# State products as 64 by 64 tiles with crossed heads, gates fetched first, single stores, weight sums on VectorE, and a new order

## The chip, the cores and the metric

One Trainium2 chip, one of its cores. The metric is the device time of one execution in microseconds (us). The matrix engine (TensorE) is called PE here, its weight loads PEld; VectorE is DVE, ScalarE is ACT, GpSimdE is POOL, and SP is the engine whose queue issues nearly all DMAs.

## What is computed

A gated linear recurrence with a complex gate (four sequences of 768 tokens, eight heads of 48), and behind it a feed-forward layer with a squared ReLU:

```python
mag = np.sqrt(a_re * a_re + a_im * a_im)
scale = np.minimum(mag, 0.999) / (mag + 1e-06)
a_re_n, a_im_n = (a_re * scale, a_im * scale)
for t in range(S):
    new_re = ar * S_re - ai * S_im
    new_im = ar * S_im + ai * S_re
    kv = np.einsum('bhd,bhe->bhde', k[:, :, t], v[:, :, t])
    S_re, S_im = (new_re + kv, new_im)
    y[:, :, t] = np.einsum('bhd,bhde->bhe', q[:, :, t], S_re)
x = y.transpose(0, 2, 1, 3).reshape(B * S, H * D)     # 3072 x 384
h = np.maximum(x @ w_in, 0.0)                          # w_in 384 x 2048
return (h * h @ w_out).astype(np.float32)              # w_out 2048 x 384
```

The weights arrive in 64-bit floating point, everything else in 32-bit.

## The kernel before

**Tiles and stages.** The tokens are cut into 24 chunks of 128. Two chunks of two sequences form a group; there are 12 groups (`NGR`), and groups 0 and 6 hold first chunks of their sequences, 5 and 11 last ones. Eight heads stand as four pairs (`NP`), the two heads of a pair on partitions 0 to 47 and 64 to 111; the fourth pair lies in the gap rows of the other three and is moved out by small DMAs.

**What a group needs.** `load_parts` (token `l`) fetches gates, queries and keys into the one buffer `raw` by 16 DMAs, `load_values` (`v`) the values. `make_operands` (`o0` to `o21`) turns gates into running quotients: ACT and DVE by turns, ending in `products` (four multiplications that write `qk`) and `last_heads` (six DMAs). `chunk` (`a` and `b`, one for each chunk of the group) makes the attention: `scores` (products of the queries with the state, L810, then the scores of keys and queries, L817, then six transposes of the keys, L824), `turned_keys` (ACT copies them), `masked` (DVE), `sums_of_values` (L845), `tokens` (ACT copies the result to `x`), `added` (L860), `new_state` (DVE) and `state_operand` (ACT spreads the new state over `state_mm`, which has zeros beside each head so that one 128-wide product does both heads of a pair). `fill_gaps` (`g`) moves the fourth pair's part of `x` into the gap rows by two DMAs, and then the feed-forward begins: eight `first_product` (`F`, L902), each followed by `squared_relu` on ACT (`H`).

**The second product.** For group 0 it is the plain one (`S`, then `E`, L918). For groups 1 to 11 it is done with seven half products in place of eight (`Z`, L975), for which DVE forms sums of the hidden values (`X`, `Y`, `Q`) and puts the results together (`R`, which also issues the stores of the output on SP in its steps 5 and 6). The sums of the weights that this needs are made once by `sum_weights` (`t`) on POOL.

**The weights.** They come as 16 blocks: `fetch` (`f`) loads one into one of three buffers, `weights` (`D`) turns it into 32-bit floats by five DVE instructions, `watch` (`W`) has ACT look at its size. The string `order` says that blocks of the first and the second matrix alternate. A feed-forward block `F` of any group needs one block of the first matrix.

**What sets the order.** The string `FRONT` is the whole order, written out token by token. The instructions of PE, DVE, ACT and SP stand on their queues exactly in that order, and each engine does its own in order; POOL is left to the scheduler. PSUM has eight banks: two each for `a_ps`, `m` (transposes and `add`) and `h`, one each for `y` and `o_ps`. A path for unusual inputs follows; it is not run here.

## Time and profile before

| | us |
|---|---|
| median of 3 runs | 794.98 (793.86 to 795.91) |
| the profiled execution, its own time | 796.23 |
| its span | 794.5 |
| PE busy | 648.3 (82%) |
| DVE busy | 544.5 (69%) |
| ACT busy | 380.9 (48%) |
| POOL busy | 25.1 (3%) |

The span is what the profiler covers from the first to the last instruction; the execution's own time is 1.7 us longer. A 32-bit matmul appears as two records, so 48 first products of a group are 96 records. A record's duration is a latency, and records overlap: what one costs in a row of many is read from the chain of waits, where a line gives the time that a run of them held the chain. The granted clock of PE is given as a share of full speed, 1.00 for 2.4 GHz and 0.50 for 1.2 GHz.

### The profile page before, as it was taken

The numbers are of one execution on the slowest core, as the hardware profiler recorded it, in microseconds if no ns is written. First come the engines' busy times: TensorE is split into PE (matmuls) and PEld (weight loads), VectorE is DVE, ScalarE is ACT, GpSimd is POOL, SyncE is SP. The second block draws the span as 40 slices with busy tenths as digits, with TensorE's granted clock in tenths as the row PEclk, the third lists the DMA queues.
The fourth block names the chain that finished last, engine by engine and source line by source line (L and its number), as shares of the span: only waits on it lengthen the run. The fifth ranks groups of instructions, "written<-read, shape, count | busy, mean of one in ns | idle before, by whom it ended". The sixth has DMA issues, their size and how long they took to land.

```text
span 794.5 us, 12035 instructions
## 1 busy us (share of the span) xinstructions
PE 648.3 (82%) x4683; PEld 585.8 (74%) x4683; DVE 544.5 (69%) x1060; ACT 380.9 (48%) x654; POOL 25.1 (3%) x38
## 2 busy tenths in 40 slices
PE   0005396887974999999996999999869979999995
PEld 0004385656974998998995999989859968989995
DVE  2899999999654697777862977868826847833120
ACT  2638547446622934828343646366337266132130
POOL 3000001050000000000000000000000000000000
PEclk9999687998996999999997999999969999999999
DMA  7567694033014143062331061430620510020001
GB/s 166 131 104 155 120 183 99 2 73 64 9 26 79 41 70 60 18 95 70 50 46 31 6 100 41 68 78 2 97 68 2 80 36 11 6 52 16 13 7 26
DMA packets 46019, 47.72 MB, mean 60 GB/s; under 512 B 5888, under 2 KB 40832, under 8 KB 45952
## 3 DMA queue, kind: packets, MB, share of 16 engines
q1 hardware_dynamic: 45440, 46.46, 31.0%
q8 instruction: 39, 0.64, 0.4%
q10 hardware_dynamic: 512, 0.39, 0.2%
q14 instruction: 28, 0.23, 0.1%
HBM read 36.18 MB, written 4.72 MB: 51 GB/s over the span
## 4 chain that ended last, share of the span: by engine, by line
PE 64%; DVE 15%; DMA 10%; ACT 4%; SPq 4%; issue 2%; ACTq 0%; DVEq 0%
PE h_ps L902 29%; PE o_ps L975 21%; DMA raw<-in_feat_dram 5%; PE a_ps L817 4%; PE y L810 4%; PE y L845 3%; DMA x<-x 2%; DVE ab L461 2%; DVE pr L461 2%; PE add L860 2%; PE tp L824 2%; DVE decoded L558 1%; DVE decoded L553 1%; DMA words<-in_moe_w_in_dram 1%; DVE w L461 1%
## 5 line engine op out<-in xcount | busy, mean ns | idle before, releaser
L902 PE MATMUL h_ps<-x,w 128*128 128x256 f32 x1152 | 270.4, 394 | 52.0 <-DMA x<-x 42.4
L902 PEld LDWEIGHTS h_ps<-x,w 128*128 128x128 f32 x1152 | 225.5, 198 | 86.9 <-issue 27.6
L975 PE MATMUL o_ps<-w,h 128*128 128x192 f32 x704 | 120.6, 328 | 0.2 <-DVE h L461 0.2
L975 PEld LDWEIGHTS o_ps<-w,h 128*128 128x128 f32 x704 | 114.6, 190 | 1.5 <-issue 0.7
L907 ACT ACTIVATE h<-h_ps 128x512 f32<-128x512 f32 x96 | 57.2, 596 | 109.4 <-PE h_ps L902 109.3
L817 PE MATMUL a_ps<-qk 48*128 48x128 f32 x576 | 42.2, 297 | 59.3 <-ACT sq L661 59.3
L817 PEld LDWEIGHTS a_ps<-qk 48*128 48x128 f32 x576 | 37.5, 204 | 62.8 <-ACT sq L661 59.6
L461 DVE TENSOR_TENSOR a<-a_ps,mask 128x512 f32<-128x512 f32 x48 | 30.8, 684 | 46.7 <-PE a_ps L817 46.7
L908 ACT ACTIVATE h<-h 128x512 f32<-128x512 f32 x96 | 60.6, 631 | 3.1
L975 PE MATMUL o_ps<-w_sum,mix 128*128 128x192 f32 x352 | 60.4, 327 | 0.0
L975 PEld LDWEIGHTS o_ps<-w_sum,mix 128*128 128x128 f32 x352 | 57.4, 190 | 0.7 <-issue 0.3
L461 DVE TENSOR_TENSOR pr<-ab 128x384 f32<-128x384 f32 x84 | 53.0, 631 | 3.4 <-ACT ab L721 0.9
L641 ACT ACTIVATE qk<-raw 128x768 f32<-128x768 f32 x24 | 36.3, 1529 | 31.4 <-DMA raw<-in_feat_dram 13.6
L461 DVE TENSOR_TENSOR mix<-h 128x256 f32<-128x256 f32 x44 | 18.5, 421 | 47.5 <-ACT h L908 47.5
L461 DVE TENSOR_TENSOR qk<-ab,qk 128x768 f32<-128x768 f32 x48 | 44.9, 956 | 0.8
L461 DVE TENSOR_TENSOR o<-o_ps,o 128x192 f32<-128x192 f32 x33 | 11.5, 354 | 44.3 <-issue 22.3
L829 ACT COPY kt<-tp 128x384 f32<-128x384 f32 x40 | 19.6, 491 | 35.2 <-PE tp L824 35.2
L641 ACT ACTIVATE both<-z 128x768 f32<-128x768 f32 x24 | 35.4, 1566 | 1.8 <-DVE z L692 1.8
L641 ACT ACTIVATE ab<-raw 128x768 f32<-128x768 f32 x24 | 35.8, 1559 | 0.0
L461 DVE TENSOR_TENSOR ab<-pr 128x192 f32<-128x192 f32 x84 | 33.2, 395 | 2.9
L845 PE MATMUL y<-a,vt 128*64 128x128 f32 x384 | 29.0, 291 | 7.5 <-DMA vt<-in_vtok_dram 4.1
L661 ACT ACTIVATE sq<-raw 128x1536 f32<-128x1536 f32 x12 | 17.7, 1478 | 35.0 <-DVE ab L461 18.6
(300 smaller groups left out, 870.0 us busy)
## 6 DMA issues: line engine op xcount, KB each, us to landing
raw<-in_feat_dram SPq DMA_DIRECT2D x44, 288.0 KB
words<-in_moe_w_out_dram SPq DMA_DIRECT2D x8, 768.0 KB
last<-qk SPq DMA_DIRECT2D x72, 64.5 KB
words<-in_moe_w_in_dram SPq DMA_DIRECT2D x16, 288.0 KB
vt<-in_vtok_dram SPq DMA_DIRECT2D x24, 192.0 KB
out_dram<-o SPq DMA_DIRECT2D x24, 192.0 KB
raw<-in_feat_dram SPq DMA_DIRECT2D x132, 32.0 KB
words<-in_moe_w_in_dram SPq DMA_DIRECT2D x16, 96.0 KB
```

The costliest lines, as they stand in the source:

```text
L461: nc.vector.tensor_tensor(out=out, in0=in0, in1=in1, op=op)
L641: nc.scalar.activation(out=out.rearrange("p c j n -> p c n j"), func=AF.Copy, in_=in_.rearrange("p c (n j) -> p c n j", j=L), **kwargs)
L661: nc.scalar.activation(out=tiles["sq"], in_=r[:, A_RE:A_IM + 1], func=AF.Square)
L810: nc.tensor.matmul(y[:, p_], rhs=operand(c, p_, slice(0, P)), lhsT=state_mm[b][:, c, p_].rearrange("p hh e -> p (hh e)"), start=(p_ == 0 a ...
L817: nc.tensor.matmul(ps[hh][:, p_], lhsT=operand(2 + c, p_, rows(hh)), rhs=operand(c, p_, rows(hh)), start=(c == RE), stop=(c == IM))
L824: nc.tensor.transpose(tp[:, g], qk[:, 2 + c, b, g, 0:C], ident)
L829: nc.scalar.copy(out=kt[c][:, 0:NG], in_=tp)
L845: nc.tensor.matmul(y[hh * ROWS:(hh + 1) * ROWS, p_], lhsT=v[:, at:at + ROWS], rhs=tiles["am"][hh][:, p_], start=(first and p_ == 0), stop= ...
L902: nc.tensor.matmul(ps[:, j], lhsT=w1[:, g, (2 * f + j) * P:(2 * f + j + 1) * P], rhs=x_of[i][:, g], start=(g == 0), stop=(g == NG - 1))
L907: nc.scalar.activation(out=h, in_=h_ps[i, f], func=AF.Relu)
L908: nc.scalar.activation(out=h, in_=h, func=AF.Square)
L975: nc.tensor.matmul(to, lhsT=x(k)[:, j], rhs=factors[z][:, 2 * k + j], start=(z in (0, 1, 3) and k == j == 0), stop=(k == KH // 2 - 1 and j ...
```

## The change

- **State products.** The product of queries with the state is no longer one 128-wide instruction for a pair of heads but one of 64 rows by 64 columns for each head. For odd pairs the two heads' outputs are crossed, so that four consecutive instructions use the four quarters of the array; even and odd pairs write two different PSUM tiles `ys`, and `py` has two banks, `pm` one. The state is kept in the layout in which PE reads it, so `state_operand` goes, and `tokens` copies two halves. The rows of the first weight matrix are crossed in the same way when they are fetched, which takes six DMAs instead of four.
- **Transposes.** They leave `scores` and become separate steps (`keys_turned`, `keys_copied`, for the real part and then the imaginary one), which share the one bank of `pm` with `add`.
- **Front.** Gates, values, queries and keys of group 0 are fetched first, the first weight block behind them. All eight blocks of the first matrix come before the eight of the second. Group 1 too gets the plain second product, block by block (`T`).
- **Weight sums.** The four subtractions go from POOL to DVE, as separate steps.
- **Stores.** They leave `R` and `E` and become steps `s`.
- **Order.** `FRONT` is new throughout.

```diff
-    py = ctx.enter_context(tc.tile_pool(name="py", bufs=1, space=PSUM))
-    pm = ctx.enter_context(tc.tile_pool(name="pm", bufs=2, space=PSUM))
+    py = ctx.enter_context(tc.tile_pool(name="py", bufs=2, space=PSUM))
+    pm = ctx.enter_context(tc.tile_pool(name="pm", bufs=1, space=PSUM))
...
+    def crossed(hh, p_):
+        at = (hh ^ p_ % 2) * ROWS
+        return slice(at, at + ROWS)
...
-    order = "1212121212121212"
+    order = "1111111122222222"
...
-            nc.gpsimd.tensor_tensor(out=out_, in0=x, in1=y, op=ALU.subtract)
...
+        tt(w2_sums[i], x, y, ALU.subtract)
...
             if not first:
-                for p_ in range(NP):
+                for two in range(0, NP, 2):
                     for c in (RE, IM):
-                        nc.tensor.matmul(
-                            y[:, p_], rhs=operand(c, p_, slice(0, P)),
-                            lhsT=state_mm[b][:, c, p_].rearrange("p hh e -> p (hh e)"),
-                            start=(p_ == 0 and c == RE), stop=False, skip_group_check=True)
+                        for hh in range(HH):
+                            for p_ in (two, two + 1):
+                                nc.tensor.matmul(
+                                    ys[p_ % 2][crossed(hh, p_), p_ // 2],
+                                    lhsT=states[b][1 - c_seq % 2][rows(hh), c, p_],
+                                    rhs=operand(c, p_, rows(hh)),
+                                    start=(p_ < 2 and c == RE), stop=False, skip_group_check=True)
...
-            nc.scalar.copy(out=x_of[gi][:, :, b * C:(b + 1) * C], in_=tiles["y"])
+            for odd in range(2):
+                nc.scalar.copy(out=x_of[gi][:, odd::2, b * C:(b + 1) * C],
+                               in_=tiles["y"][odd][:, 0:NP // 2])
...
-        def state_operand():
-            for hh in range(HH):
-                nc.scalar.copy(out=state_mm[b][rows(hh), :, :, hh, 0:D], in_=state[n][rows(hh)])
...
+    def store(i, b):
+        nc.sync.dma_start(out=in_turn(out, groups[i][b]), in_=out_of[i, b])
...
-        "M0 f0 D0 W0 l0.0 o0.0 o0.1 o0.3 o0.4 o0.5 o0.2 o0.7 o0.8 o0.10 o0.9 f1 W1 f2 W2 D1 "
+        "M0 l0.0 v0 v1 l0.1 o0.0 o0.3 o0.1 o0.4 o0.5 o0.7 o0.2 f0 o0.8 o0.10 o0.9 o0.11 o0.6 W0 "
```

How the order moves is shown at three places, as the instructions stand on an engine's queue.

**DVE at the last weight block.** First before, then now. `decoded` and `w_59` are a block of the second weight matrix being turned into floats; `a` is masked scores of group 1, `both`, `ab`, `sq` and `raw` gates of group 2 before, and of group 3 now.

```order
L551 TENSOR_SCALAR decoded<-words 128x768
L553 SCALAR_TENSOR_TENSOR decoded<-words,decoded 128x768
L555 TENSOR_SCALAR decoded<-decoded 128x768
L558 SCALAR_TENSOR_TENSOR decoded<-words,decoded 128x768
L461 TENSOR_TENSOR w_59<-decoded 128x768
L461 TENSOR_TENSOR a<-a_ps,mask 128x512 x2
L713 SCALAR_TENSOR_TENSOR both<-both 128x768
L461 TENSOR_TENSOR ab<-ab,both 128x1536
L717 SCALAR_TENSOR_TENSOR sq<-z,sq 128x768
L727 SCALAR_TENSOR_TENSOR sq<-sq 128x128 x6
```

```order
L478 TENSOR_TENSOR sq<-sq 128x768
L714 SCALAR_TENSOR_TENSOR z<-sq,z 128x768
L569 TENSOR_SCALAR decoded<-words 128x768
L571 SCALAR_TENSOR_TENSOR decoded<-words,decoded 128x768
L573 TENSOR_SCALAR decoded<-decoded 128x768
L576 SCALAR_TENSOR_TENSOR decoded<-words,decoded 128x768
L478 TENSOR_TENSOR w_59<-decoded 128x768
L478 TENSOR_TENSOR w_sum<-w_59 128x1536
L735 SCALAR_TENSOR_TENSOR both<-both 128x768
L478 TENSOR_TENSOR ab<-ab,both 128x1536
```

The last block stood before the rest of group 2's operands and the second chunk of group 1; now it stands behind them and behind the first steps of group 3, and the first sum of weights follows it on DVE.

**PE at the second of group 2's chunks, up to that group's first products.** First before, then now, from the last of the new state products on. `y<-qk` and `y<-last` are state products, `a_ps` scores, `tp` transposes, `y<-a` sums of values, `add` what the chunk adds to the state, `o_ps` the second product of group 1, `h_ps` the first product of group 2.

```order
L810 MATMUL y<-qk_125,state_mm_134 128x128 x6
L810 MATMUL y<-last_127,state_mm_134 128x128 x2
L817 MATMUL a_ps<-qk_125 128x128 x12
L817 MATMUL a_ps<-last_127 128x128 x4
L824 MATMUL tp<-ident,qk_125 128x128 x6
L975 MATMUL o_ps<-w_59,h 128x192 x8
L845 MATMUL y<-a,vt_104 64x128 x8
L860 MATMUL add<-vt_104,kt_141 64x48 x8
L860 MATMUL add<-vt_104,kt_142 64x48 x8
L975 MATMUL o_ps<-w_sum,h 128x192 x8
L902 MATMUL h_ps<-x,w_58 128x256 x48
```

```order
L833 MATMUL y<-qk_125,state_134 64x128
L833 MATMUL y<-last_127,state_134 64x128
L841 MATMUL a_ps<-qk_125 128x128 x12
L841 MATMUL a_ps<-last_127 128x128 x4
L848 MATMUL tp<-ident,qk_125 128x128 x6
L867 MATMUL y<-a,vt_103 64x128 x8
L885 MATMUL add<-vt_104,kt_145 64x48 x8
L885 MATMUL add<-vt_104,kt_146 64x48 x8
L923 MATMUL h_ps<-x,w_58 128x256 x36
```

The blocks of group 1's second product that stood between scores and sums of values are gone from here; all of that product now stands ahead of both chunks. Eight 128-wide state products of a chunk have become 16 of 64 columns.

**SP at the gap rows of group 8.** First before, then now. `raw` and `vt` are loads for a later group, `out_dram` stores of the output, `x<-x` the two DMAs that fill the gap rows, `last` the six DMAs of the fourth pair.

```order
L476 DMA raw<-in_feat_dram 48x4x384
L481 DMA raw<-in_feat_dram 16x4x128 x3
L491 DMA vt_103<-in_vtok_dram 128x1x384
L491 DMA vt_104<-in_vtok_dram 128x1x384
L934 DMA out_dram<-o 8x16x384 x2
L896 DMA x<-x 16x3x256 x2
L778 DMA last_128<-qk_126 16x8x129 x6
L491 DMA vt_105<-in_vtok_dram 128x1x384
```

```order
L493 DMA raw<-in_feat_dram 48x4x384
L498 DMA raw<-in_feat_dram 16x4x128 x3
L508 DMA vt_103<-in_vtok_dram 128x1x384
L508 DMA vt_104<-in_vtok_dram 128x1x384
L917 DMA x<-x 16x3x256 x2
L962 DMA out_dram<-o 8x16x384 x2
L800 DMA last_128<-qk_126 16x8x129 x6
```

The fill of the gap rows stood behind two stores of the group before; now it stands ahead of the two stores, still behind the 16 loads of `raw` and the two of `vt`. On PE three half products of the group before (24 of the 128x192 instructions) stand between the fill and the first product that needs it.

## Rows read from the trace of the kernel before

**Rows 1.** Busy time by stage: stretch, then us of each engine, granted clock, DMA.

```profile
0.00:182.00 182.00, 85.40 (x529) 67.78 (x529) 157.81 (x252) 95.16 (x160) 22.58 (x28) 0.91 0.58 116
182.00:248.80 66.80, 50.84 (x420) 46.60 (x421) 40.52 (x84) 30.23 (x52) 0.28 (x1) 0.88 0.24 45
248.80:302.00 53.20, 51.43 (x397) 47.27 (x397) 41.62 (x87) 28.97 (x54) 0.28 (x1) 0.97 0.28 48
302.00:786.20 484.20, 460.60 (x3338) 424.12 (x3338) 304.38 (x638) 226.25 (x390) 1.96 (x8) 0.97 0.23 43
786.20:794.50 8.30, 0.03 (x2) 0.00 (x0) 0.15 (x1) 0.26 (x1) 0.00 (x0) 0.79 0.23 59
```

**Rows 2.** PE's waits from 248 us on: us in total, times, longest.

```profile
PE h_ps L902 <- DMA x<-x: 32.4, 5, 14.8
PE a_ps L817 <- DMA last<-qk: 7.8, 2, 6.8
```

**Rows 3.** Timeline at group 8's gap rows: start, us, instruction, idle before and releaser.

```profile
574.83 1.52 ACT L641 ACTIVATE qk<-raw 128x768 f32<-128x768 f32 x1 [7.92 <-DMA raw<-in_feat_dram]
...
578.91 1.42 SPq L934 DMA_DIRECT2D out_dram<-o  x2
580.38 1.34 SPq L896 DMA_DIRECT2D x<-x  x2
...
583.91 8.45 PE L902 MATMUL h_ps<-x,w 128*128 128x256 f32 x25 [10.07 <-DMA x<-x]
```

**Rows 4.** Busy time by stage, the first 20 us.

```profile
0.00:20.00 20.00, 0.48 (x1) 0.18 (x1) 4.37 (x11) 5.25 (x9) 6.02 (x22) 1.00 0.79 166
```

**Rows 5.** Chain of waits up to 200 us: start, us, what.

```profile
136.93 4.20 DVE sq L674
...
153.57 0.96 DVE w L461
...
166.15 3.70 DVE pr L461
```

**Rows 6.** DVE groups of the operands: busy us, mean ns, idle before.

```profile
L461 DVE TENSOR_TENSOR pr<-ab 128x384 f32<-128x384 f32 x84 | 53.0, 631 | 3.4 <-ACT ab L721 0.9
L461 DVE TENSOR_TENSOR qk<-ab,qk 128x768 f32<-128x768 f32 x48 | 44.9, 956 | 0.8
L461 DVE TENSOR_TENSOR ab<-pr 128x192 f32<-128x192 f32 x84 | 33.2, 395 | 2.9
L727 DVE TENSOR_TENSOR_SCAN sq<-sq 128x128 f32<-128x128 f32 x72 | 24.0, 403 | 0.2
```

**Rows 7.** Chain of waits at group 2's first products.

```profile
248.81 22.38 PE h_ps L902 x96
```

**Rows 8.** Chain of waits later: start, us, PE's runs of records.

```profile
271.19 1.78 PE y L810 x16
272.98 1.99 PE a_ps L817 x32
...
278.37 1.02 PE y L845 x16
...
329.47 2.79 PE h_ps L902 x12
...
353.65 1.07 PE add L860 x32
...
404.22 2.59 PE h_ps L902 x12
406.81 2.60 PE o_ps L975 x16
...
583.91 16.00 PE h_ps L902 x60
```

**Rows 9.** ACT groups of the chunks: busy us, mean ns, idle before.

```profile
L882 ACT COPY state_mm<-state 48x384 f32<-48x384 f32 x40 | 20.3, 507 | 14.0 <-DVE state L461 13.7
L829 ACT COPY kt<-tp 128x384 f32<-128x384 f32 x40 | 19.6, 491 | 35.2 <-PE tp L824 35.2
```

More of the change, by code (lines that the diff above doesn't have):

```diff
@@ L54, in w1_views @@
     rest = w[cut:].rearrange("(hh r g) f -> hh r g f", hh=HH, g=groups)
-    return [(head_rows(hh, d), main[hh]) for hh in range(HH)] + [
-        (gap_rows(hh, d), rest[hh]) for hh in range(HH)]
+    if not crossed:
+        return [(head_rows(hh, d), slice(0, groups), main[hh]) for hh in range(HH)] + [
+            (gap_rows(hh, d), slice(0, groups), rest[hh]) for hh in range(HH)]
+    assert groups % 2
+    return [(head_rows(hh, d), slice(odd, groups, 2), main[hh ^ odd][:, odd::2])
+            for hh in range(HH) for odd in range(2)] + [
+        (gap_rows(hh, d), slice(0, groups), rest[hh ^ groups % 2]) for hh in range(HH)]
 def w2_view(w):
@@ L98, in decode_weights @@
                 decode(w1[:, g, f], words, 512)
+    else:
+        for rr, _, src in w1_views(w_in, d):
+            nc.sync.dma_start(out=w1[rr], in_=src)
     if w_out.dtype != F32:
@@ L105, in decode_weights @@
             decode(w2[:, fb], words, width)
+    else:
+        nc.sync.dma_start(out=w2, in_=w2_view(w_out))
 @with_exitstack
@@ L523, in quotient_path @@
         nc.gpsimd.memset(t[:, :, :, :, C:W], 0.0)
-    state_mm = [const.tile([P, 2, NP, HH, ROWS], F32, name=f"state_mm{i}") for i in range(GC)]
-    for t in last + prod + state_mm:
+    states = [[const.tile([P, 2, NP, ROWS], F32, name=f"state{b}{i}") for i in range(2)]
+              for b in range(GC)]
+    for t in last + prod + states[0] + states[1]:
         nc.gpsimd.memset(t, 0.0)
@@ L581, in fetch @@
             else:
-                for at, src in w1_views(w_in, D):
-                    nc.sync.dma_start(out=w1[at, :, f], in_=src[:, :, f])
+                for at, gs, src in w1_views(w_in, D, crossed=True):
+                    nc.sync.dma_start(out=w1[at, gs, f], in_=src[:, :, f])
             return
@@ L819, in scores, with keys_turned, keys_copied @@
                                          stop=(c == IM))
-            tiles["tp"] = []
-            for c in () if final else (RE, IM):
-                tp = pm.tile([C, NG, P], F32, tag="m", name="tp")
-                for g in range(NG):
-                    nc.tensor.transpose(tp[:, g], qk[:, 2 + c, b, g, 0:C], ident)
-                tiles["tp"].append(tp)
-        def turned_keys():
-            for c, tp in enumerate(tiles["tp"]):
-                nc.scalar.copy(out=kt[c][:, 0:NG], in_=tp)
-                nc.scalar.copy(
-                    out=kt[c][:, NG].rearrange("t (hh x) -> t hh x", hh=HH)[:, :, 0:D].rearrange(
-                        "t hh (r g) -> t hh g r", g=NG),
-                    in_=tp.rearrange("t g (hh x) -> t hh g x", hh=HH)[:, :, :, D:ROWS])
+        def keys_turned(c):
+            tp = tiles["tp"] = pm.tile([C, NG, P], F32, tag="m", name="tp")
+            for g in range(NG):
+                nc.tensor.transpose(tp[:, g], operands[gi][:, 2 + c, b, g, 0:C], ident)
+        def keys_copied(c):
+            tp = tiles["tp"]
+            nc.scalar.copy(out=kt[c][:, 0:NG], in_=tp)
+            nc.scalar.copy(
+                out=kt[c][:, NG].rearrange("t (hh x) -> t hh x", hh=HH)[:, :, 0:D].rearrange(
+                    "t hh (r g) -> t hh g r", g=NG),
+                in_=tp.rearrange("t g (hh x) -> t hh g x", hh=HH)[:, :, :, D:ROWS])
         def masked():
@@ L863, in new_state @@
         def new_state():
-            new = state[n] = att.tile([P, 2, NP, D], F32, name="state", bufs=3)
+            before, new = [states[b][i][:, :, :, 0:D] for i in (1 - c_seq % 2, c_seq % 2)]
             if first:
@@ L868, in new_state @@
                 sum_ = new
-                tt(sum_, tiles["add"], state[n - 1], ALU.add)
+                tt(sum_, tiles["add"], before, ALU.add)
             pd = prod[gi % 2][:, :, b]
@@ L922, in block_of_second @@
         if f == 0:
-            for b, (pool, tag) in enumerate(((po, "o"), (py, "y"))):
+            pool, tag = (py, "y") if i == 0 else (pa, "a")
+            for b in range(GC):
                 o_of[i, b] = pool.tile([P, DM], F32, tag=tag, name="o_ps")
@@ L931, in quarter_of_second @@
         second_product(i, b, every[q * QUARTER:(q + 1) * QUARTER])
-    def store(i, b, o, queue):
-        queue.dma_start(out=in_turn(out, groups[i][b]), in_=o)
+    out_of = {}
     def end_of_second(i, b):
-        o = ffn.tile([P, DM], F32, name="o")
-        nc.scalar.copy(out=o, in_=o_of[i, b])
-        store(i, b, o, nc.sync)
+        out_of[i, b] = ffn.tile([P, DM], F32, name="o")
+        nc.scalar.copy(out=out_of[i, b], in_=o_of[i, b])
+    def store(i, b):
+        nc.sync.dma_start(out=in_turn(out, groups[i][b]), in_=out_of[i, b])
     def sums_of_halves(i, k):
```

59 lines of the change are left out of this document (30 added, 29 removed), and 125 rows, old and new, of the table FRONT.

## The prediction

> **What bounds the kernel now.** I read the busy time by stage first [rows 1], then who PE waits for [rows 2], then the places of the longest waits in the timeline [rows 3] and the chain of waits [rows 5, 7, 8]. The stages have different limits. Up to 182 us DVE is busy 157.8 of 182 us and PE 85.4: DVE turns weights and prepares operands, PE waits for both. DVE is idle mainly at the start, with 4.4 us busy of the first 20 [rows 4]. From 302 us on PE is busy 460.6 of 484.2 us, DVE 304.4 and ACT 226.3: PE is the bound, and its work plus its holes is the time. The stage between is mixed. So I cut the span at the first product of group 2, at 248.8 us [rows 7]: ahead of it everything hangs on DVE's order, behind it (248.8 to 786.2, 537.4 us) on PE's work, and after 786.2 the tail is 8.3 us [rows 1].
>
> PE's holes behind 248.8: waits for the fill of the gap rows come to 32.4 us in 5, the longest 14.8; that one lies just ahead of group 2's first product, which leaves 17.6. Waits for the fourth pair's DMAs add 7.8 [rows 2]. Together 25.4 us. Each long hole also lowers the clock: after the one at 583.9, 60 records of first products hold the chain for 16.00 us where 12 take 2.59, so 12.95 [rows 8], 3.0 us lost. I put all the half-clock stretches behind the remaining holes (25 us of waits, the 10.1 us one costing 3.0) at 6 us, an estimate.
>
> Rows 3 show what makes such a hole. ACT waits 7.92 us for `raw`; the copies of the output stand behind that on ACT, two stores wait for these copies on SP, and the fill of the gap rows stands behind the stores. PE then waits 10.07 us.
>
> **The front.** The last weight block is finished at 154.5 us (153.57 + 0.96) [rows 5]. The new order puts more DVE work ahead of it and takes none away: the rest of group 2's operands, the second chunk of group 1, the first steps of group 3. From the totals of 12 groups: 53.0/12 + 44.9/12 + 33.2/12 + 24.0/12 = 12.9 us for the four largest kinds [rows 6], and some 12.5 for the rest of the same steps (three gate operations, one product with the keys, the totals of a block, six operations with the carries), which makes 25.4; masks and state of one chunk 3.4; group 3's first steps 3.1. That is 32 us. On the other side POOL's sums of weights go: one DVE operation at 136.9 took 4.20 us beside them, and another at 166.2 took 3.70 against a mean of 0.63 [rows 5, 6]. Only the first of these lies ahead of the last block, about 3 us. At the same idle time at the start the last block is done at 154.5 + 32 - 3 = 183.5. The idle time: the gates now arrive ahead of the weights, but nothing fills DVE's waits for ACT in group 0's chain, so I leave it as it is and take 5 us either way.
>
> Behind that block PE has two blocks of the plain second product, each as long as 16 records of 192 columns, 2.60 us [rows 8]. That gives 189; PE itself is nearly full from the eighth block on (first products of group 1, 8 x 2.6, and 16 blocks of second products, 16 x 2.6, with a chunk), so I take 191. Then group 2's two chunks follow, nothing between them: the PSUM banks for their scores are held by the second products until ACT has copied those. State products 0.9, scores 2.0, mask 1.3, sums of values 1.0, `add` 1.1, and once more without `add` (the durations by [rows 8]), then the copies to `x` 0.8, the fill 0.7 to issue and 3 to land, with about 3 us for hand-overs: some 19 us. First product of group 2 at 210, with 203 to 225 as bounds. That is **38.8 us earlier** than 248.8. It contains the one change that makes PE's work longer: a plain second product for group 1, 16 x 2.6 = 41.6 us for two groups. Before, PE did this work in the stretch in which it now waits for the chunks.
>
> **State products.** Of 20 chunks with a state, 16 lie behind group 2's first product. Before, 16 records hold the chain 1.78 us, 0.111 each. The sums of values are 64 columns wide, so that two of them fill the array's 128 columns: 16 records of as many columns take 1.02 us, 0.064 each [rows 8]. So two tiles of 64 columns do run beside each other. The 32 new records of a chunk use four; if all four run, that is 8 rounds of 0.111, 0.9 us. The change into another tile shape costs about 0.2: 12 records of first products take 2.79 us behind such a change and 2.59 without [rows 8]. Gain per chunk 1.78 - 0.9 - 0.2 = 0.7, by 16 chunks **11 us**. Bounds: four tiles without the cost of a change give 14; if only two run, 16 rounds are 1.8 us and it loses 0.2 a chunk, 3 us; if none overlaps, 32 x 0.111 = 3.5 us and it loses 31.
>
> The Trainium skill, "TensorEngine Tiling (Array Packing)", section Restrictions and Gotchas, says that different row tiles cannot access the same PSUM bank simultaneously. Here the two heads of a pair are two row tiles, and they write the two halves of one bank; the scores, whose row tiles write one bank each, do not show such a case. By that rule only two tiles run, the case priced above; it is a rival below.
>
> **PE's holes.** In the new order the fill of the gap rows stands ahead of the stores, and three half products, 3 x 2.60 = 7.8 us [rows 8], lie between it and the first product that needs it. The `raw` loads ahead of it on SP still take about 8.5 us to issue, and then the loads of values 1.4 and the fill itself 1.4; by counting the blocks from the last copy of the keys, which frees `raw`, PE has about 18 us of work there and the chain needs 14 to 15. So the 25.4 us of waits and 6 us of clock go. I do not believe that nothing takes their place: group 3's fourth pair is still late by a microsecond or two, and 0 to 16 us in all are possible. I put 8 back: **23 us** gained. About 7 changes of tile shape more than those counted above, at 0.2, cost 1.
>
> **Edits that cost nothing.** ACT loses 40 copies of 0.51 us, 20 us [rows 9], and gains some 4 for `tokens` in two halves; it is busy 226 of 484 us, so neither shows. DVE gets four sums of weights, about 1.8 us each, of which two fall behind group 2's first product, where DVE has 53.2 - 41.6 = 11.6 us free [rows 1]. If that cover were gone, 3.6 us. Six DMAs instead of four for a block of the first matrix are 16 more on SP in the front, about 0.6 us each; DVE, not the fetch, is late there, and if it were the fetch, up to 8 us of the 32 would come on top; the bound of 225 holds this.
>
> **The sum**, from the profiled execution: 796.2 - 38.8 - 11 - 23 + 1 = 724.4. The median of the runs is 1.2 below the profiled one, so **723 us**. With the bounds: 203 us for group 2, no new holes and 14 for the tiles give 704; 225 us and 16 us of holes give 746.
>
> **The rivals.**
> - *Two tiles instead of four.* For it: no row shows row tiles in one bank. Against it: each quarter has its own partitions of the bank. The state products gain nothing: 723 + 14 = 737, and with no overlap at all 723 + 42 = 765. This is also the case in which the change doesn't do what it says.
> - *The fill stays late.* 16 loads of `raw` still stand ahead of it on SP, and PE's cover beyond the chain is only 3 to 4 us. If each of the nine groups loses 2.5 us and 1.5 of clock, 36 us less the 8 already counted: 751, up to 765. For it: all long waits of before are of this kind [rows 2]. Against it: the stores, which made them long, are gone from ahead.
> - *The front gains nothing.* Group 2's two chunks now stand alone on PE, at a falling clock, with DVE's operands of group 3 between their masks. If group 2 starts where it did, 723 + 39 = 762.
> - *Slower: one bank for transposes and sums.* `pm` has one bank instead of two, so that in each chunk three uses wait for one another: real transposes, imaginary ones, `add`, each freed by ACT or DVE. Behind group 2's start that is 3 x 16 = 48 hand-overs. If ACT stands behind one squared ReLU (1.23) and then copies (0.49 [rows 9] and a smaller one of 0.3), PE loses 2 us at each, 96 in all: 819. It decides the sign from 1.5 us a hand-over on (72/48). Against it: between two uses PE has a block of 2.6 us or a chunk's scores in nearly every place, which hides 2.0.
>
> **How the numbers follow.** Forecast, 704 to 746: 0.63. Two tiles or none: 0.12. Late fill: 0.12. Front without gain: 0.08. Slower: 0.03. Faster than 704: 0.02. The predicted time is the forecast's, 723. The range 704 to 752 holds the forecast, the two tiles and about half of the late fill, and leaves out 0.19. A measurement of this kernel tells 0.3% (2.4 us) from no change; no case but the slower one comes near or above 793, so faster 0.96, within 0.01, slower 0.03.
>
> **What would show it.** In the changed profile: the last weight block on DVE ends at 180 to 190 us; group 2's first product starts near 210; 32 records of state products hold the chain about 0.9 to 1.1 us (1.8 if two tiles); PE's waits for `x<-x` behind that start are below 10 us; the stretch from it to the last product is about 500 us instead of 537; no group waits more than 1 us for `tp` or `add`'s bank. Wrong would be a period above 54 us from one group's first product to the next, or a start of group 2 above 225.

## The result, and the profile after

The changed kernel takes 719.69 us, median of 4 runs (718.32 to 722.88), beside 795.44 us for the kernel before (4 runs, 793.86 to 796.08): ratio 0.9056, 95% interval 0.9023 to 0.9089. The profiled execution is the one of 718.32 us, with a span of 716.5.

Busy time by stage of the changed kernel (stretch, us of PE, PEld, DVE, ACT, POOL, granted clock, DMA share, GB/s). The third line ends and the fourth begins at the first product of group 2; the fourth ends with the last product.

```profile
0.00:40.00 40.00, 0.48 (x1) 0.18 (x1) 14.25 (x29) 18.90 (x25) 6.11 (x24) 1.00 0.48 109
40.00:182.00 142.00, 103.53 (x685) 79.71 (x686) 136.98 (x232) 88.41 (x155) 2.04 (x3) 0.95 0.62 124
182.00:215.50 33.50, 27.28 (x280) 19.09 (x278) 30.37 (x51) 13.31 (x26) 0.00 (x0) 0.99 0.46 76
215.50:708.70 493.20, 492.79 (x3990) 448.80 (x3990) 350.00 (x735) 247.70 (x432) 3.74 (x9) 1.00 0.25 46
708.70:716.50 7.80, 0.07 (x2) 0.00 (x0) 0.15 (x1) 0.30 (x1) 0.00 (x0) 0.80 0.18 52
```

Group 2 starts at 215.5 where it started at 248.8 [rows 1, 7]. From there to the last product it is 493.2 us instead of 537.4, and in these PE is idle for 0.4 us: the steady part has no hole left, at a mean granted clock of 1.00 (0.97 before). So of the 78 us between the two profiled spans 33.3 were gained in the front, 44.2 behind it, 0.5 in the tail. PE's waits from 215 us on, which answer to [rows 2] (total, times, longest); the first is the one ahead of group 2's first product itself:

```profile
PE h_ps L923 <- DMA x<-x: 3.2, 1, 3.2
PE y L833 <- DMA last<-qk: 0.4, 1, 0.4
```

The chain of waits at two chunks of the steady part, which answers to [rows 8] (start, us, what): the 32 state products take 1.03 us where 16 took 1.78; scores and sums of values are as before, and `add` takes 1.07 behind scores and 0.92 behind sums of values; 12 records of first products take 2.79 behind a change of tile shape and 2.59 without, as before.

```profile
239.79 1.07 PE add L885 x32
240.86 2.79 PE h_ps L923 x12
243.64 1.02 PE y L867 x16
...
247.47 1.03 PE y L833 x32
248.50 1.99 PE a_ps L841 x32
...
254.92 0.92 PE add L885 x32
...
261.23 2.59 PE h_ps L923 x12
```

Where the 44.2 us went is seen best by summing, over all PE records of the stretch, the time from the start of one to the start of the next, by the operation of the earlier one (a wait is counted with the record ahead of it). The last two columns are for runs described below, `uncrossed` and `old_order`.

| us from group 2's first product to the last | before | after | uncrossed | old_order |
|---|---|---|---|---|
| state products | 30.0 | 17.3 | 32.4 | 17.1 |
| scores | 45.0 | 35.7 | 35.7 | 45.0 |
| transposes of keys (`tp`) | 10.6 | 10.6 | 10.6 | 30.4 |
| sums of values, `add` | 31.7 | 32.4 | 32.4 | 31.7 |
| first products | 216.9 | 210.9 | 210.0 | 222.7 |
| second products | 203.0 | 186.1 | 186.4 | 204.8 |
| sum | 537.3 | 493.1 | 507.7 | 551.8 |

State products gave 12.7. The other 31.5 are the holes (scores and second products: the waits for `last` and for `x<-x` stand behind them) and the half clock that followed them (first products; the granted clock is 0.97 before and 1.00 after).

The front, by the chain of waits ahead of group 2:

```profile
183.86 9.69 PE o_ps L939 x30
193.58 0.49 ACT o L959
194.08 3.88 DMA out_dram<-o
198.06 0.49 ACT o L959
198.59 1.10 PE y L833 x30
199.68 2.04 PE a_ps L841 x32
201.72 1.27 DVE a L478 x2
```

The second products of groups 0 and 1 run without a break up to 196.1. What was not foreseen is the step behind them: the four outputs share a tile `o` of two buffers, so the copies of group 0's outputs wait for the stores of group 1's to land, and group 2's state products, whose bank the copies free, wait for these. The last weight block and ACT's waits (start, us, idle before and releaser):

```profile
188.74 0.96 DVE L478 TENSOR_TENSOR w<-decoded 128x768 f32<-128x768 f32 x1
...
196.24 0.48 ACT L959 COPY o<-o_ps 128x384 f32<-128x384 f32 x1 [1.42 <-DMA out_dram<-o]
...
198.06 0.48 ACT L959 COPY o<-o_ps 128x384 f32<-128x384 f32 x1 [1.34 <-DMA out_dram<-o]
```

### The profile page after: what moved, and what is told of

It reads as the page before. It is cut to its first block, busy times and chain, and to the rows that moved or that the text cites. A ratio compares the mean times of both kernels' runs of the same rounds, so it can differ in the third digit from the quotient of the medians.

```text
span 716.5 us, 12546 instructions
## 1 busy us (share of the span) xinstructions
PE 624.1 (87%) x4955; PEld 547.8 (76%) x4955; DVE 531.7 (74%) x1045; ACT 368.6 (51%) x636; POOL 11.9 (2%) x36
## 4 chain that ended last, share of the span: by engine, by line
PE 73%; DVE 13%; DMA 7%; SPq 3%; issue 1%; ACT 1%; ACTq 0%; DVEq 0%
PE h_ps L923 29%; PE o_ps L998 26%; PE a_ps L841 5%; PE o_ps L939 5%; DMA raw<-in_feat_dram 4%; PE y L867 2%; PE y L833 2%; DVE ab L478 2%; PE add L885 2%; PE tp L848 1%; DMA words<-in_moe_w_in_dram 1%; SPq L800 1%; DVE pr L478 1%; DVE w L478 1%; DVE qk L478 1%
## 5 line engine op out<-in xcount | busy, mean ns | idle before, releaser
L923 PE MATMUL h_ps<-x,w 128*128 128x256 f32 x1152 | 261.0, 384 | 8.8 <-DMA x<-x 8.0
L923 PEld LDWEIGHTS h_ps<-x,w 128*128 128x128 f32 x1152 | 219.1, 193 | 39.9 <-DMA x<-x 5.4
L998 PE MATMUL o_ps<-w,h 128*128 128x192 f32 x640 | 110.3, 328 | 0.0
L998 PEld LDWEIGHTS o_ps<-w,h 128*128 128x128 f32 x640 | 104.0, 190 | 2.2 <-issue 1.5
L848 PE MATMUL tp<-ident,qk 128*128 128x128 f32 x120 | 22.2, 297 | 62.9 <-DVE qk L478 54.7
L848 PEld LDWEIGHTS tp<-ident,qk 128*128 128x128 f32 x120 | 14.7, 148 | 68.4 <-ACT size L584 55.0
L998 PE MATMUL o_ps<-w_sum,mix 128*128 128x192 f32 x320 | 54.9, 329 | 0.0
L998 PEld LDWEIGHTS o_ps<-w_sum,mix 128*128 128x128 f32 x320 | 51.8, 190 | 1.4 <-issue 1.4
L478 DVE TENSOR_TENSOR pr<-ab 128x384 f32<-128x384 f32 x84 | 46.8, 557 | 2.3
L939 PE MATMUL o_ps<-w,h 128*128 128x384 f32 x128 | 42.3, 488 | 1.2 <-DVE w L478 0.6
L939 PEld LDWEIGHTS o_ps<-w,h 128*128 128x128 f32 x128 | 24.2, 190 | 17.5 <-DVE w L478 1.3
```

What stands on the lines that cost most here:

```text
L478: nc.vector.tensor_tensor(out=out, in0=in0, in1=in1, op=op)
L848: nc.tensor.transpose(tp[:, g], operands[gi][:, 2 + c, b, g, 0:C], ident)
L923: nc.tensor.matmul(ps[:, j], lhsT=w1[:, g, (2 * f + j) * P:(2 * f + j + 1) * P], rhs=x_of[i][:, g], start=(g == 0), stop=(g == NG - 1))
L939: nc.tensor.matmul(o_of[i, b], lhsT=tokens_of(i, f, b)[:, j], rhs=w2[:, k], start=(k == 0), stop=(k == NFB - 1))
L998: nc.tensor.matmul(to, lhsT=x(k)[:, j], rhs=factor(z)[:, 2 * k + j], start=(z in (0, 1, 3) and k == j == 0), stop=(k == KH // 2 - 1 and j ...
```

## The experiments

Twelve kernels ran, all of them the changed kernel with one edit or two. A letter and a number in the order are a step of the plan: `g5` the fill for group 5, `s4.0` a store of group 4, `a7.1` the real keys turned in the first chunk of group 7 (.2 copied, .3 and .4 the imaginary ones), `l4` the loads of `raw` for group 4, `f0 D0 W0` fetch, turning and sizes of the first weight block. For each run I name two times of its profile: the start of group 2's first product ("cut", 215.5 after) and the stretch from there to the last product (493.1 after).

**Only two of the four tiles** (`uncrossed`).

```diff
-        at = (hh ^ p_ % 2) * ROWS
+        at = hh * ROWS
...
-                for at, gs, src in w1_views(w_in, D, crossed=True):
+                for at, gs, src in w1_views(w_in, D):
```

> The heads of odd pairs are not crossed: each head's product of the state reads and writes its own 64 rows and columns, so only two of the four tiles of 64 by 64 are used; everything else, the order too, is that of the changed kernel. Theory (four tiles run beside each other): 32 records of state products hold PE about 1.8 us a chunk where they took 1.03, so 0.77 x 16 = 12 us more behind group 2's first product and 1 to 3 in front of it: 731 to 735 us. Rival (the shorter records are a matter of the half as wide tiles, not of the crossing): the 32 records stay at about 1.0 us and the time at 718 to 721. Rival (the products of two row tiles wait for one another at the bank in any case): the same, no change.

Measured: 735.47 us (ratio to before 0.9274, 0.9245 to 0.9302), cut 216.8, stretch 507.7. A chunk in its chain of waits:

```profile
249.27 1.95 PE y L833 x32
251.22 1.99 PE a_ps L841 x32
```

The theory holds (the time is 0.5 us above its range): 1.95 instead of 1.03, and the table above shows that the whole difference of the stretch, 14.6 us, is in the state products (32.4 against 17.3). Without the crossing the 64 by 64 form is worse than the form before (30.0): the gain hangs on all four tiles.

**The order of the 32** (`same_tile_twice`).

```diff
-                    for c in (RE, IM):
-                        for hh in range(HH):
-                            for p_ in (two, two + 1):
+                    for hh in range(HH):
+                        for p_ in (two, two + 1):
+                            for c in (RE, IM):
```

> The same 32 state products of a chunk on the same four tiles, in another order: the real and the imaginary product of one tile stand directly behind each other, where before all four tiles came in turn. Theory (products run beside each other only where neighbours in the order use different tiles): pairs of neighbours wait for each other, so that a chunk takes 1.5 to 1.9 us instead of 1.03, 0.5 to 0.9 x 16 = 8 to 14 us more: 727 to 734 us. Rival (PE looks far enough ahead, the order within the 32 is free): 1.0 to 1.1 us and 718 to 721.

Measured: 721.36 us (719.15 to 721.86), stretch 494.7, and `249.46 1.10 PE y L833 x32` in the chain of waits. The theory falls, the rival holds: with two neighbours on one tile a chunk costs 0.07 us more, 18.7 against 17.3 us in the stretch.

**The fill behind the store** (`fill_behind_store`).

```diff
-  ... v7 g5 Z4.4 R4.3 o6.17 Z4.5 R4.4 o6.18 Z4.6 R4.5 s4.0 o6.19 o7.6 F5.0 ...
+  ... v7 Z4.4 R4.3 o6.17 Z4.5 R4.4 o6.18 Z4.6 R4.5 s4.0 g5 o6.19 o7.6 F5.0 ...
```

> For seven groups (4 to 9 and 11) the fill of the gap rows stands on SP directly behind the first store of the group before, no longer ahead of it, still ahead of the first product that reads it. Theory (the place of the fill on SP is what took PE's waits for x<-x away): the fill now waits with the store for the output's copies; PE has one half product of 2.6 us left between them and the fill needs 0.7 to issue and 3 to land, so PE waits 2.5 to 5 us a group and loses 1 to 1.5 of clock behind it: 7 x 3.5 to 6.5 = 25 to 45 us more, 743 to 765 us, with PE waits for x<-x of 18 to 35 us in all (8.0 in the changed kernel). Rival (the waits went since the half products and chunks are spread better, and the copies of the output come early enough): waits below 10 us and 718 to 724.

Measured: 743.39 us (742.78 to 745.94), stretch 515.7. PE's waits from the cut on, and one of the seven places in the chain of waits:

```profile
PE h_ps L923 <- DMA x<-x: 20.0, 8, 2.8
```

```profile
424.60 0.66 SPq L917
...
425.31 2.48 DMA x<-x
...
427.93 13.19 PE h_ps L923 x60
```

The theory holds at the low end of its range. Seven new waits of 1.8 to 2.8 us make 17.4; the sums by operation show 18.6 more in the second products and 4.0 in the first products, where the granted clock fell behind two of the waits (0.59 over 481 to 485 us, 0.72 over 692 to 698); together the 22.6 of the stretch. The place of the fill on one DMA queue, in seven groups, is worth half of what was gained behind the cut.

**Sums of weights on POOL** (`pool_sums`).

```diff
-        tt(w2_sums[i], x, y, ALU.subtract)
+        nc.gpsimd.tensor_tensor(out=w2_sums[i], in0=x, in1=y, op=ALU.subtract)
```

> The four sums of weights go back to POOL, at the same places of the order. Theory (beside a POOL operation DVE's operations on two tensors take several times as long, and DVE sets the end of the front): the two sums at 190 us slow the few DVE operations beside them, the first chunk's masks and the operands of group 3 among them, by 2 to 8 us in all: group 2's first product at 217 to 222 instead of 215.5, and 720 to 727 us; the two later ones at 217 are covered or cost 1 to 2. Rival (PE's chain of chunk steps, not DVE, sets the end there): 717 to 719, or up to 3.5 us faster, as DVE is rid of two operations of 1.75 us ahead of the masks.

Measured: 726.87 us (726.31 to 728.4), cut 224.0, stretch 493.7. The timeline, POOL and then the DVE operations beside it:

```profile
175.38 4.14 POOL L630 TENSOR_TENSOR w_sum<-w 128x1536 f32<-128x1536 f32 x1 [4.25 <-DMA words<-in_moe_w_out_dram]
192.71 3.94 POOL L630 TENSOR_TENSOR w_sum<-w,w_sum 128x1536 f32<-128x1536 f32 x1 [13.19 <-DVE w L478]
196.59 4.96 POOL L630 TENSOR_TENSOR w<-w 128x1536 f32<-128x1536 f32 x1
```

```profile
176.15 4.18 DVE L696 SCALAR_TENSOR_TENSOR sq<-sq 128x768 f32<-128x768 f32 x1
193.38 4.88 DVE L478 TENSOR_TENSOR ab<-ab,both 128x1536 f32<-128x1536 f32 x1
198.18 4.19 DVE L739 SCALAR_TENSOR_TENSOR sq<-z,sq 128x768 f32<-128x768 f32 x1
```

The theory holds, at the upper end of its time and with the cut beyond its 217 to 222; the loss is in the front, the stretch is as in the changed kernel. There these DVE operations take 0.95, 1.76 and 0.95 us. Beside POOL each ends behind the POOL operation that it started beside, by a little less than its own length: at 180.3 behind 179.5, 198.3 behind 196.7, 202.4 behind 201.6. The Trainium skill, "SBUF — State Buffer", section "SBUF: two separate sides", says that a GpSimd operation that reads SBUF and a VectorE operation with two SBUF inputs share a port pair, that the one that starts first holds it for its whole length, and that the other fully blocks. Those three ends agree.

**Four buffers for the output tile** (`o_bufs4`).

```diff
-        out_of[i, b] = ffn.tile([P, DM], F32, name="o")
+        out_of[i, b] = ffn.tile([P, DM], F32, name="o", bufs=4)
...
```

The same edit stands at the second place that takes this tile.

> The tile of the output has four buffers instead of two. Theory (the copies of group 0's outputs wait at 194.7 to 198.1 us for the stores of group 1's to land, 1.4 and 1.3 us, and group 2's state products wait for those copies): both waits go, the state products start at 195 to 196 instead of 198.6, group 2's first product comes 2 to 3.5 us earlier, at 212 to 213.5: 715 to 717 us. Rival (DVE's masks, not PE's state products, are last there): under 1 us, 717.5 to 719.5.

Measured: 718.64 us (717.67 to 719.32; ratio to before 0.9049, 0.9032 to 0.9066), not told apart from the changed kernel. Both waits are gone and the state products start at 196.5, but the cut comes at 214.5, only 1.0 earlier. SP, then ACT:

```profile
208.92 1.77 SPq L498 DMA_DIRECT2D raw<-in_feat_dram  x3
210.79 1.28 SPq L917 DMA_DIRECT2D x<-x  x2
```

```profile
209.43 0.65 ACT L876 COPY x<-y 128x256 f32<-128x256 f32 x2 [0.53 <-PE y L867]
```

The tokens are copied at 210.1; SP takes the fill behind the last of 16 loads of `raw`. Neither the theory nor its rival (the masks): another wait was next in line.

**Those loads behind the fill** (`o4_loads_late`), on top of the four buffers.

```diff
-  ... o3.15 a2.4 l4 a2.8 b2.7 ... a2.7 g2 b2.9 v4 ...
+  ... o3.15 a2.4 a2.8 b2.7 ... a2.7 g2 l4 b2.9 v4 ...
```

> Four buffers for the output's tile, and the loads of group 4's gates on SP behind the fill of group 2's gap rows, no longer ahead of it. With the four buffers alone the state products started 2.1 us earlier, but the first product of group 2 came at 214.5, only 1.0 earlier: the chunk's tokens were done at 210.1, and SP took the fill at 210.8, behind the last of 16 loads that ended at 210.7. Theory (those loads now set the fill): it is issued at 210.1 and lands sooner as nothing else is under way, first product at 212 to 213.5, 716.5 to 717.8 us. Rival (the tokens set it as much): 0 to 0.7 us, 718 to 718.6.

Measured: 725.98 us (725.54 to 727.72), cut 214.2, stretch 501.2. The fill goes out as soon as the tokens are copied (211.16):

```profile
211.18 1.32 SPq L917 DMA_DIRECT2D x<-x  x2
```

The last weight block ended at 190.9 in this run and at 189.8 in the one with the four buffers alone; from the block to the cut it is 23.3 us here and 24.7 there. So the theory's first half holds, with some 1.4 us. But the loads now come too late for ACT's copy of `raw`, behind which the squared ReLUs of group 2 stand, and PE has a new wait:

```profile
PE h_ps L923 <- ACT h L928: 6.9, 1, 6.9
```

**The first weights ahead of the gates** (`weights_first`).

```diff
-  M0 l0.0 v0 v1 l0.1 o0.0 ... o0.2 f0 o0.8 ... o0.6 W0 f1 ... f2 D0 o0.18 ...
+  M0 f0 D0 W0 l0.0 v0 v1 l0.1 o0.0 ... o0.2 o0.8 ... o0.6 f1 ... f2 o0.18 ...
```

> The first block of weights is fetched and turned ahead of the gates again, as in the kernel before (its fetch, its operations on DVE and its sizes on ACT stand first); the rest is the changed kernel. In the first 40 us DVE was busy 21.3 us in the kernel before and 14.3 in the changed one. Theory (DVE's idle time at the start passes on to the last weight block, which came at 189.7 us, 6 later than forecast): DVE does some 4 us of the weights' work before the gates arrive, the last block ends 3 to 7 us earlier, and the time falls to 713 to 717 us. Rival (fetching the gates first is what the order gains by: they come 4 to 5 us later here, and DVE, which has nothing else then, loses as much as it gained): 718 to 724 us.

Measured: 719.7 us (715.11 to 721.76), the same as the changed kernel. Busy time by stage:

```profile
0.00:40.00 40.00, 0.48 (x1) 0.18 (x1) 17.86 (x33) 19.25 (x25) 6.12 (x24) 1.00 0.46 107
40.00:182.00 142.00, 104.97 (x690) 79.97 (x691) 135.11 (x229) 89.02 (x157) 1.31 (x3) 0.94 0.61 125
...
197.00:203.00 6.00, 5.93 (x64) 5.38 (x65) 1.25 (x2) 2.14 (x5) 0.00 (x0) 0.52 0.62 135
```

DVE does 3.6 us more by 40 us, and half of that is lost again by 182; the last weight block ends at 188.2 instead of 189.7. Eight profiled runs with the changed kernel's own front (without `pool_sums`) have it from 189.4 to 190.9, and the two further runs below with the weights first at 189.6 and 187.9, so the 1.5 us are of the size of the spread. In the profiled run PE then ran the state products and scores of group 2's first chunk at half clock (0.52) behind its wait for the copies of `o`, and group 2 started at 217.1. The theory holds for DVE in part; the time is the rival's. But the six runs differ in their mean granted clock: five lie at 0.974 to 0.979 and take 719.4 to 721.8 us, one has 0.986 and takes 715.11, where the changed kernel's run at 0.986 takes 718.32. So the lower clock may hide a gain of some 3 us; one run doesn't show it.

**Both** (`o4_weights_first`): the edits of `o_bufs4` and of `weights_first`.

> The two changes of the front that each left the time as it was, together: four buffers for the output's tile, and the first block of weights ahead of the gates. Alone, the second had the last weight block 1.5 us earlier, but PE, which still waited 1.7 us for the copies of group 0's outputs, ran the scores behind that at half clock (3.71 us instead of 2.04), and group 2 started at 217.1. Theory (the wait and the half clock behind it ate the gain): the state products start at 195 or earlier, group 2's first product at 212.5 to 213.5, 2 to 3 us earlier than in the changed kernel: 716 to 718 us. Rival (the fill behind group 4's loads is last in any case): first product at 214 to 215.5, 718 to 720 us.

Measured: 715.56 us (713.15 to 718.52), ratio to before 0.8992 (0.8972 to 0.9011), below the changed kernel's 0.9056 (0.9023 to 0.9089): some 4 us, 0.6%, the best version found. But the profiled run is the slowest of its five (718.52), with the cut at 214.5, as in the rival. Where the other four gained is not seen in a trace of theirs. In the profiled one DVE waited 1.9 us for `add`, and the last weight block ended at 189.6; in the next run, with the same order up to there, it ended at 187.9:

```profile
DVE state L478 <- PE add L885: 1.9, 1, 1.9
```

```profile
186.94 0.96 DVE L478 TENSOR_TENSOR w<-decoded 128x768 f32<-128x768 f32 x1
```

So 1.7 us of the gain may come and go with that. The half clock ahead of group 2 also comes and goes: with the changed kernel's own front and two buffers the profiled cut was 215.5 to 216.9 in three runs, whose scores took 2.03 or 2.04 us, and 218.2 to 218.8 in three others, whose scores took 3.72 to 3.76 (`pool_sums` left out).

**Half of the loads behind the fill** (`o4_loads_split`), on top of that version: `l4` in its place for the first chunk, behind `g2` for the second.

```diff
-        for b, n in enumerate(groups[gi]):
+        for b, n in list(enumerate(groups[gi]))[part == 4:1 if part == 3 else GC]:
...
-  ... a2.4 l4 a2.8 ... a2.7 g2 b2.9 ...
+  ... a2.4 l4.3 a2.8 ... a2.7 g2 l4.4 b2.9 ...
```

> The version with four output buffers and the first weights ahead of the gates (715.6 us), and of group 4's 16 loads of gates the second chunk's 8 behind the fill of group 2's gap rows on SP; there the tokens were done at 209.9 us, the last load issued at 210.8, the fill issued at 211.1, the first product of group 2 at 214.5. Theory (SP's loads hold the fill by 1.2 us; half of them behind it are early enough for the copies on ACT, which needed them at 214): the fill is issued at 209.9 to 210, the first product starts at 213 to 213.5, and the time falls by 1 to 1.5 to 714 to 715 us. Rival (the loads come too late for ACT, whose copy of raw then holds the squared ReLUs behind it, as where all 16 were moved): 717 to 723 us with a PE wait for h of 2 to 5 us.

Measured: 717.85 us (716.22 to 718.09), cut 211.3, stretch 496.4. SP, then ACT, then PE's new wait:

```profile
208.22 1.31 SPq L917 DMA_DIRECT2D x<-x  x2
```

```profile
217.69 1.50 ACT L663 ACTIVATE qk<-raw 128x768 f32<-128x768 f32 x1 [9.50 <-DMA raw<-in_feat_dram]
```

```profile
PE h_ps L923 <- ACT h L928: 3.5, 1, 3.5
```

The first half of the theory holds: the fill goes out as soon as the tokens are there, at 208.2, and group 2 starts 3.2 us earlier, of which 1.7 are the earlier weight block. The rival decides the time: ACT's copy of `raw` waits until 217.7 with the squared ReLUs behind it, and PE gives 3.5 us back. The time is not told apart from that of `o4_weights_first`: the ratios to before are 0.9011 (0.8991 to 0.9032) and 0.8992 (0.8972 to 0.9011).

**The changed code in the old order** (`old_order`): the order of the kernel before, written with the new steps (the real keys turned behind the scores; their copies, the imaginary transposes and copies where the copies stood; stores behind their outputs).

> The changed kernel's code (four tiles, one bank for transposes and sums, two for outputs of the chunks, weights' sums on DVE) in the order of the kernel before: same first stages, group 1 by half products, the fill of the gap rows behind the stores, the real keys turned with the scores and the imaginary ones behind their copies. Theory (the tiles give about 12 us, the order the rest, and the one bank costs little): 0.75 x 16 to 20 = 12 to 15 us below the kernel before, less 0 to 8 for hand-overs of the bank in an order that was not made for it: 780 to 790 us. Rival (the one bank costs 1.5 us and more at each hand-over unless the order provides for it): PE waits for tp and add of 30 to 70 us in all and 800 to 850 us. Rival (most of the gain comes from the code, the order adds little): 720 to 750.

Measured: 810.93 us (809.58 to 813.42), ratio 1.0189 (1.0169 to 1.0209): slower than the kernel before. PE's waits over the whole span:

```profile
PE h_ps L923 <- DMA x<-x: 41.3, 7, 15.5
PE tp L848 <- ACT kt L853: 33.7, 19, 5.4
PE a_ps L841 <- DMA last<-qk: 10.4, 4, 7.0
```

The column of the table above tells it: behind the cut (251.6) the state products gave their 12.9, and the transposes took 19.8 more (30.4 against 10.6), since real and imaginary ones share the one bank, stand directly behind each other in most chunks and wait for ACT's copies (16.6 of the 33.7 us lie there). The holes of the old order stayed (31.3 us of waits for fills and 7.7 for `last`, against 32.4 and 7.8), and first products lost 5.8, at a granted clock of 0.96. The theory misses by the bank; the first rival is right in kind, and its 800 to 850 in size. Written so, the edit of the code alone loses; the order makes it gain. The front too is the order's: the cut is 2.8 us later than in the kernel before, not 33.3 earlier.

**Keys turned together** (`keys_together`, then `keys_adjacent`): in 14 steady chunks the imaginary transposes moved up, first directly behind the real copies, then copies and imaginary transposes both directly behind the real transposes.

```diff
-  ... a7.1 F6.6 o8.7 a7.2 H6.2 o8.8 b7.0 H6.6 X6.2 o8.10 a7.3 ... a7.4 ...
+  ... a7.1 F6.6 o8.7 a7.2 a7.3 H6.2 o8.8 b7.0 H6.6 X6.2 o8.10 ... a7.4 ...
```

> In 14 chunks behind group 2's start (groups 3 to 10 without the last of a sequence) PE turns the imaginary keys directly behind the real ones; in the changed kernel a block of first products or a chunk's scores lies between. Both write the one bank, so the second must wait for ACT's two copies of the first (0.48 and 0.30 us). Theory (one bank is free of cost only since the order puts other work of PE between two uses; this, with the late fill, is what made the changed code slower than the kernel before in the old order): PE waits 0.8 us at each where ACT is free and up to 2.3 where it is in the middle of something else, 14 x 0.8 to 2.3 = 11 to 32 us more: 731 to 752 us, and PE waits for tp on ACT of 15 to 36 us in all (4.2 in the changed kernel). Rival (PE's later work closes up, or the holes in the old order have other causes): below 5 us, 718 to 725.

Measured: 726.54 us (722.07 to 727.69), stretch 497.3, 4.2 more. The edit did less than its text says: in all 14 chunks PE still had other work between the two transposes, a block of 2.6 us in eight (`F6.6` above) and sums of values of 1.0 us in six. PE's waits from 216 us on:

```profile
PE tp L848 <- ACT kt L853: 3.4, 6, 0.6
```

Those six wait, behind sums of values each time, and the eight do not: a block of 2.6 us covers the hand-over, 1.0 us does not. The second form leaves nothing between.

```diff
-  ... a7.1 F6.6 o8.7 a7.2 H6.2 o8.8 b7.0 H6.6 X6.2 o8.10 a7.3 ...
+  ... a7.1 a7.2 a7.3 F6.6 o8.7 H6.2 o8.8 b7.0 H6.6 X6.2 o8.10 ...
```

> The run before this one moved the imaginary keys behind the copies of the real ones, but on PE a block of work still stood between the two in about half of the 14 chunks; it cost 4.2 us behind group 2's start (493.1 to 497.3), with waits of 0.6 us at most. Here the real transposes, their copies and the imaginary transposes follow each other directly in all 14 chunks, with nothing between on PE. Theory (the one bank costs wherever nothing covers ACT's copies): 14 waits of 0.8 to 1.0 us where ACT is free and 1.5 to 2.5 where it is in the middle of a squared ReLU, 14 x 0.8 to 2.5 = 11 to 35 us: the stretch from group 2's first product to the last one at 504 to 528 us, the time at 731 to 755. Rival (a hand-over costs a few tenths, as in that run): 497 to 501 us for the stretch, 723 to 729.

Measured: 735.1 us (732.0 to 735.93), stretch 506.9. PE's waits from 216 us on:

```profile
PE tp L848 <- ACT kt L853: 11.3, 14, 1.4
```

14 waits of 0.8 us, 13.8 us in the stretch (1.0 a hand-over): the theory, near its low end. The sum by operation puts 13.6 of it on the transposes (24.2 against 10.6).

## Why the prediction was right, and what in it was not

The time came out at 719.69 against 723, inside the forecast's own range, with its mechanism. Two of its terms were off, in opposite directions: group 2's start was put 5.5 us too early, and the stretch behind it 11.2 us too long. That the time is within 3.3 us is in part luck, since the two offset each other.

- **Last weight block: 189.7, forecast 183.5.** The step that failed is "I leave it as it is", of DVE's idle time at the start. In the first 40 us DVE was idle 25.75 us after (40 less 14.25 in the first table); in the kernel before it was busy 21.29 there, idle 18.71. That is 7.0 us more, and the block came 6.2 later. The first 20 us were read for the amount of idle time [rows 4], not for what DVE did in its 4.4 busy us: 4.0 of them were the first weight block, which the new order takes behind the gates. Up to the end of the block DVE was busy 131.4 of 154.5 us before and 158.7 of 189.7 after: 27.3 more work, where 32 less 3 was put, and 7.9 more idle. The lines, of the kernel before and then of the changed one:

```profile
0.00:40.00 40.00, 0.48 (x1) 0.18 (x1) 21.29 (x34) 18.26 (x26) 6.02 (x22) 1.00 0.65 148
0.00:154.50 154.50, 64.17 (x444) 54.06 (x445) 131.41 (x211) 85.35 (x141) 11.79 (x25) 0.90 0.62 123
```

```profile
0.00:189.70 189.70, 111.71 (x710) 84.46 (x711) 158.72 (x269) 112.13 (x185) 8.15 (x27) 0.96 0.57 116
```

This is an account of where the time lies. That filling the start brings the block back by as much is not shown: `weights_first` gave DVE 3.6 us there, and its block came 1.5 earlier.

- **Group 2 at 215.5, forecast 210.** PE's second products end at 196.1 where 191 was forecast, all of it the block's delay; the 19 us for the two chunks behind them are 19.4. They contain a wait that the prediction had not seen (the two buffers of `o`); taking it away gave 1 us, since group 4's loads on SP are nearly as late, and moving those gave some 1.4. So -33.3, not -38.8, inside the bounds.
- **State products: -12.7, forecast -11.** All four tiles run: 1.03 us for 32 records, where 0.9 and 0.2 were put; 1.95 with two. The rival of two tiles falls. With it falls, for this case, the rule that the Trainium skill states in "TensorEngine Tiling (Array Packing)", section Restrictions and Gotchas: two row tiles wrote the two halves of one bank and did not exclude each other, or no more than two of the four could have run at a time. 1.03 lies 0.14 above eight rounds of 0.111 and 1.95 0.17 above sixteen, near the 0.2 put for the change of tile shape; no run takes that change apart.
- **Holes: -31.5, forecast -23.** The size of the holes and of their clock (31.4) was right; the 8 us put back for waits in their place never came. PE waits 0.4 us behind the cut. The cause named, the place of the fill on SP, is borne out: moving it behind the first store in seven groups brings 22.6 back. How the 17.6 us of old waits divide between that place and the cover on PE, and what ended the waits for `last`, no run takes apart. The rival of a late fill falls as well: the cover was enough in every group, though the three half products of the forecast stand only in groups 4 to 9 (two in group 3, one in 10 and 11).
- **Costless edits.** ACT's saved copies and DVE's sums show nowhere behind the cut, where PE waits 0.4 us. The sums were worth something in the front, by not being on POOL (7 us).
- **The slower rival, one bank for transposes and sums.** In this order no hand-over behind the cut waits, so it did not come. But it was the right thing to weigh: 0.8 to 1.0 us a hand-over where nothing covers ACT's copies, 0.6 where 1.0 us of PE's work covers part of them, and in the old order 19.8 us, which with the holes left in place made the same code slower than the kernel before. The prediction's "between two uses PE has a block of 2.6 us or a chunk's scores in nearly every place" is a statement on the order, not on the code.

What stays open: which part of the new order makes the 33.3 us of the front, the largest gain (the blocks of the first matrix ahead of the second, group 1's plain second product, or group 2's operands ahead of the last block; the sum of the prediction accounts for them together, and no run takes one of them back); where the four unprofiled runs of `o4_weights_first` gained, and what an order would give that takes ACT's copy of `raw` for group 4 behind group 2's first squared ReLUs, so that the fill may go ahead of all the loads (group 2 at 211.3 without the 3.5 us given back); it was not tried.

## What to carry to other kernels

Cost an edit of buffers and the order that hides it as one thing: the one bank was free in the new order and cost 20 us of transposes in the old one. When an order moves work out of a stage's idle start, ask what that engine did there: here its idle time grew by 7 us, and the last weight block came 6 us later than forecast. And when the wait that ends last is taken away, list what ends next and on which queue: behind the four buffers stood the loads on SP, and behind those ACT's copy, and each took back most or all of what the step before had won.

## What was not expected of the hardware

- Four tiles of 64 by 64, with two row tiles writing the two halves of one bank: 32 records in 1.03 us, two tiles 1.95. With neighbours on the same tile 1.10, so the order within the 32 hardly matters.
- Behind two waits of PE of 0.3 and 1.4 us, at 195 to 200 us, the granted clock fell to the lower of its two levels in some runs (0.54 over 198 to 208 us of `keys_together`; 3.72 us for 32 score records instead of 2.04) and not in others with the same order up to there (1.00 over the same stretch of `uncrossed`). Group 2 started at 218.2 to 218.8 with it and at 215.5 to 216.9 without.
- DVE's operations on two tensors beside a POOL operation on two tensors ended only behind it, by nearly their own length: 4.18 and 4.88 us beside POOL's 4.14 and 3.94, for 0.95 and 1.76 alone.
